# Another order of one unit's tiles, of its tails' preparation, and another issuer of one load

## The chip, the cores and the metric

The kernel runs on one core of one Trainium2 chip. The metric is the device time of one execution in microseconds; of the kernel before there are three runs, and their median is taken.

## The reference

Three stages follow one another. Attention has 4 batches, 8 heads, 576 positions and 64 elements a head, with a causal mask and a bias that decays with a cumulated sum. A sticky top-1 mixture of experts (512 inputs, 1024 hidden) and a gated convolution block with two further matrix products come behind it.

```
scores = scale * np.matmul(q, k.transpose(0, 1, 3, 2))
cum = np.cumsum(np.maximum(s, 0.0), axis=-1)
bias = -(cum[:, :, :, None] - cum[:, :, None, :])
scores = np.where(causal, -1000000000.0, scores + np.minimum(bias, 0.0))
attn = np.exp(scores - np.max(scores, axis=-1, keepdims=True))
attn = attn / (np.sum(attn, axis=-1, keepdims=True) + 1e-09)
x = np.matmul(attn, v)                      # heads beside one another
...
e = fresh_e if s == 0 or local_gate[b, s] < 0.5 else prev_e   # per token
out[b, s] = p[e] * (np.maximum(x[b, s] @ w1[e], 0.0) @ w2[e])
...
h = np.maximum(x @ w_in, 0.0)
y = (h * sigmoid(conv3(h, conv_w))) @ w_out
```

## The kernel before

The change touches attention alone, and there its beginning. The 32 pairs of batch and head are worked off as 8 units of 4 heads. Of the 576 positions 512 are the main part, laid out as transposed operands (`K1`, and `k2` in the second half of the contraction), and 64 are the tail, whose operands for all heads lie in `T1` and `T2`. Numbers are split into a high and a low float16 part, so a score tile is a sum of products of parts.

A unit has 14 score tiles (h, g). Tiles with g = 0, g = 1, and g = 2 of even heads need main operands only; g = 2 of odd heads and g = 3 need the tail operands as well. The order of the tiles of a unit is fixed: head 0 with g = 0, 1, 2, head 1 with g = 0 to 3, and the same for heads 2 and 3. Only unit 0 has an order of its own, the list `BEGIN`.

The main loop `for t in range(N + 9)` (L722) takes one tile a step. In step t it does what is planned for the step (`work`), the scores of tile t on PE into PSUM (L482, with masks L485), the pieces of the row maxima of a coming unit (`stage_a`: PE L382, then DVE L385 or, for tails, L413), the exps of tile t − 1 on ACT (`weights`: L521, or L526 and L527), the low part of the weights of tile t − 2 on DVE (`plo`, L538), and products with V four steps behind the last tile of a head (`values`, L554, started for an odd head by its tile g = 3, for an even one by g = 2). Output of a pair of heads is normalised, split and stored five to seven steps behind, and turned on PE by identity matmuls 10, 12 and 14 steps behind the tiles (1, 3) and (3, 3) (`turn_tile`, PE L914, emptied by ACT L915).

Row maxima are needed before the scores of a unit: PE turns them (L450, `max_turn`), ACT scales them (L455), and a DMA writes them into an operand row. They and `turn_tile` use the PSUM pool `mps`, which has one buffer; the pieces have two (`aps`), score tiles three (`zps`).

What is prepared ahead is planned by the table `PAR`: each name in `start` has a step, negative ones come before the loop, and equal steps go by the fraction. The names of the tails' chain are `thk`, `thq` (high parts, ACT), `tlk`, `tlq` (low parts, DVE L293), `ttk`, `ttq` (turned on PE L298, out by L301 on ACT and L303 on DVE), `ct` (copies into T1, DVE L327), `xt` (three operand rows, DMA), `pt` (the tail pieces of unit 0's maxima), `mtt`, `mot`, `mrt` (the maxima turned, scaled and written; `mrt` is a DMA on ACT's queue, L465). For unit 1: `hk1`, `hq1`, `lk1`, `lq1` (splits, ACT L259 and DVE L265), `T1k`, `T1q` (DMA transposes L277 on SP), `x1`, and its copies (L285, DVE) in `copies`; in `u1`, `sv` is the split of V, `pa` and `pn` the first step of the pieces and the number of steps they are spread over. `lk2`, `lq2` load q and k of unit 2, whose splits run on ACT (L259) and POOL (L267, L268). `lv0` and `lv1` load the two halves of V of batch 0 (`loadv`, L176 and L180), `sv0` splits the first (ACT L342, DVE L346, POOL L337 to L350), `c2` writes constants (POOL L205), `z` writes zeros.

Every engine, and SP's and POOL's queues too, works in the order in which the program issues, and waits at an instruction until its operands are there.

Of the kernel before, what the change touches and what calls it, by code (L numbers as in the profile page):

```python
# [42 lines left out]
class Keep:  # L43
# [3 lines left out]

PAR = {'u1': {'sv': -6, 'pa': -6, 'pn': 4, 'mx': -3},  # L50
 'u2': {'at': (-22, -21, -19, -18.9, -18), 'cp': (-14, -13), 'lv': -11, 'sv': -2, 'pa': -12, 'pn': 7, 'mx': -6},
 'u3': {'load': -35, 'loadq': 0, 'at': (-33, -30, -28, -27, -26.9), 'cp': (-22, -21), 'sv': -1, 'pa': -20, 'pn': 14, 'mx': -6},
 'u': {'load': -51,
# [34 lines left out]
           'hk1': -17,  # L88
           'mob': -16,
           'mrb': -15,  # L90
           'tlk': -14,
           'tlq': -13,
           'lk1': -12,
           'xt': -11,
           'T1k': -10,
           'ttk': 2.0,
           'ttq': 3.0,
           'hq1': 3.05,
           'lq1': 3.06,
           'T1q': 3.07,  # L100
           'x1': 3.08,
           'lk2': 3.09,
           'lq2': 3.095,
           'ct': 4.0,
           'pt': 4.1,
           'c2': 4.5,
           'mtt': 5.0,
           'mot': 5.1,
           'mrt': 5.2,
           'sv0': 5.4,  # L110
           'z': 6.0,
           'lv1': 6.1},
 'r': {'cut': 12, 'w1': 6, 'w2': 8, 'w3': 22},
 'm': 'faafaafaafaa'}


BEGIN = ([(0, 0), (0, 1), (1, 0), (1, 1), (0, 2), (1, 2), (1, 3)],
         [(0, 0), (0, 1), (1, 0), (1, 1), (2, 0), (2, 1), (0, 2), (1, 2), (1, 3), (3, 0), (3, 1), (2, 2), (3, 2), (3, 3)])


def attention(tc, ctx, q, k, v, s, xd, rt, hook):
# [8 lines left out]
    V, A, PE, Q, G = nc.vector, nc.scalar, nc.tensor, nc.sync, nc.gpsimd  # L130

    def pool(n, b, on=ctx, **kw):
        return on.enter_context(tc.tile_pool(name=n, bufs=b, **kw))

    const, vp, natv = pool("const", 1), pool("vv", 2), pool("natv", 1)
    p0p, php, wk, xp, xtp = pool("p0", PAR["h"]["p0"]), pool("phl", PAR["h"]["ph"]), pool("wk", 2), pool("xs", 2), pool("xt", 1)
    zps, aps, ops, mps = (pool(n, b, space=PSUM) for n, b in (("zps", 3), ("aps", 2), ("ops", 2), ("mps", 1)))
# [23 lines left out]
    def load(u, n):  # L161
        b, h0 = u // (H // NH), u % (H // NH) * NH
        t = big[n == "q"][:, 0:1024] if u % 2 == 0 else big[1][:, 1024 + 1024 * AT[n]:2048 + 1024 * AT[n]]
        t = U[u, n] = t.rearrange("p (h c d) -> p h c d", h=NH, c=2)
        for c in range(2):
            Q.dma_start(t[:, :, c], src[n][b, h0:h0 + NH, 256 * c:256 * c + 256].rearrange("h (p t) d -> p h (t d)", t=2))

    def loadv(b, part=None, D=Q):
        if part in (None, 0):
            U[b, "v"] = natv.tile([128, H, 4, 64], F32, name="nv")  # L170
            U[b, "vt"] = natv.tile([128, H // 2, 64], F32, name="nvt")
        w, wt = U[b, "v"], U[b, "vt"]
        h = slice(0, H) if part is None else slice(NH * part, NH * part + NH)
        for j in range(4):
            for t in range(2):
                D.dma_start(w[64 * t:64 * t + 64, h, j], v[b, h, 128 * j:128 * j + 128].rearrange("h (p t) d -> t p h d", t=2)[t])  # L176
        for e in range(2):
            for t in range(2):
                r = 64 * e + 32 * t
                D.dma_start(wt[r:r + 32, h.start // 2:h.stop // 2], v[b, h, 512:576].rearrange("(r e) (p t) d -> e t p r d", e=2, t=2)[e, t])  # L180
# [93 lines left out]
    def turn(u, e, ns=slice(0, 2)):  # L274
        if (u, 2) not in U:
            U[u, 1], U[u, 2] = K1[u % 3], st2.tile([128, 2, 2, 1024], F16, name="k2")
        Q.dma_start_transpose(out=U[u, 2][:, e, ns].rearrange("d n (x p) -> d (n x) p", p=64), in_=U[u, "h"][64 * e:64 * e + 64, ns].rearrange("p n x y d -> p (n x y d)"))  # L277
# [34 lines left out]
    def turn_tail(n, js, engines):  # L312
        for j, copy in zip(js, engines):
            turned(ht, AT[n], j, lambda z, j: (T2[:, :, AT[n], 128 * j:128 * j + 128].rearrange("d b (x p) -> d b x p", p=32), z.rearrange("d (x b p) -> d b x p", x=4, b=B)), copy)
# [14 lines left out]
    def split_v(u):  # L329
        b, o = u // 2, u % 2 * NH  # L330
        a, t = U[b, "v"][:, o:o + NH], U[b, "vt"][:, o // 2:o // 2 + 2]
        w = U[u, "vv"] = vp.tile([128, NH, 4, 2, 65], F16, name="vv")
        wt = U[u, "vvt"] = vp.tile([128, NH // 2, 2, 65], F16, name="vvt")
        v0 = U[u, "v0"] = vp.tile([128, NH, 65], F32, name="v0")
        for x in (w, wt):
            i = (slice(None),) * (len(x.shape) - 2)
            G.memset(x[i + (0, slice(64, 65))], 1.0)  # L337
            G.memset(x[i + (1, slice(64, 65))], 0.0)
        G.memset(v0[:, :, 64:65], 1.0)
        for x, dh, dl in ((a, w[:, :, :, 0, 0:64], w[:, :, :, 1, 0:64]), (t, wt[:, :, 0, 0:64], wt[:, :, 1, 0:64])):  # L340
            if u == 0 or not PAR["h"]["vg"]:
                A.activation(dh, x, AF.Copy, scale=VS)  # L342
            else:
                G.tensor_scalar(dh, x, VS, 0.0, op0=ALU.mult, op1=ALU.add)
            if u == 0:
                V.scalar_tensor_tensor(dl, in0=x, scalar=VS, in1=dh, op0=ALU.mult, op1=ALU.subtract)  # L346
            else:
                G.tensor_scalar(x, x, VS, 0.0, op0=ALU.mult, op1=ALU.add)
                G.tensor_tensor(dl, x, dh, op=ALU.subtract)
        G.tensor_scalar(v0[:, :, 0:64], a[:, :, 0], VS if u == 0 else 1.0, 0.0, op0=ALU.mult, op1=ALU.add)  # L350
# [93 lines left out]
    def max_turn(u, hs=slice(0, 4), tails=True):  # L444
        t = U[u, "mt"] = mps.tile([128, 512], F32, name="mt")
        r = span(hs, tails)
        x = mxs[u][:, 0:18] if hs == slice(0, 4) else mxs[u][:, 16:18]
        if hs and not tails:
            x = mxs[u][:, 4 * hs.start:4 * hs.stop]
        PE.matmul(t[0:r.stop - r.start, 0:128], lhsT=x, rhs=ident, start=True, stop=True, skip_group_check=True)  # L450

    def max_out(u, hs=slice(0, 4), tails=True):
        n = span(hs, tails).stop - span(hs, tails).start
        mr = U[u, "mr", key(hs)] = wk.tile([18, 128], F16, name="mr")
        A.activation(mr[0:n], U[u, "mt"][0:n, 0:128], AF.Copy, scale=2.0 ** -12)  # L455

    def max_row(u, hs=slice(0, 4), tails=True):
        n, Q = 0, nc.sync if u or hs else nc.scalar
        if hs:
            n = 4 * (hs.stop - hs.start)  # L460
            for e in range(2):
                Q.dma_start(U[u, 1][70:71, e, 1, 256 * hs.start:256 * hs.stop].rearrange("o (x c) -> o x c", c=128), U[u, "mr", key(hs)][n // 2 * e:n // 2 * e + n // 2])
        if tails:
            c = 256 * (u % 2)
            Q.dma_start(T1[70:71, u // 2, 1, c:c + 256].rearrange("o (r c) -> o r c", r=2), U[u, "mr", key(hs)][n:n + 2])  # L465
# [3 lines left out]
    def mode(x):  # L469

        m = PAR["m"][3 * x[1] + x[2]] if x[2] < 3 else "a"
        return "a" if m == "b" and x[0] < 3 else m
# [131 lines left out]
    def store(u, part):  # L604
# [3 lines left out]
        xh, eng = U[u, "xh"][:, part], G if u < NU - 1 else V  # L608
        if eng is G and PAR["h"]["xg"]:
            G.tensor_copy(xh[:, :, 0], x)  # L610
# [40 lines left out]
    copy(0, "q")  # L651
    load_tail("q")
    load(1, "k")
    todo, pieces, copies = {}, {}, {6: [(1, "k")], 7: [(1, "q")]}

    def plan(t, f):
        todo.setdefault(math.floor(t), []).append((t, len(todo), f))
# [13 lines left out]
    def second_a(r):  # L671
# [8 lines left out]
        pa=begin_a, mt0a=lambda: max_turn(0, first, False), mo0a=lambda: max_out(0, first, False), mr0a=lambda: max_row(0, first, False),  # L680
        ttk=lambda: turn_tail("k", range(4), "AVAV"), ttq=lambda: turn_tail("q", range(4), "AVAV"),
        pb=lambda: second_a(range(6, 8)), pc=lambda: second_a(range(8, 10)), pd=lambda: second_a(range(10, 12)),
        mtb=lambda: max_turn(0, second, False), mob=lambda: max_out(0, second, False), mrb=lambda: max_row(0, second, False),
        xt=extra_tail, ct=copy_tail, ldq1=lambda: load(1, "q"), lk2=lambda: load(2, "k"), lq2=lambda: load(2, "q"),
        T1k=lambda: [turn(1, e, slice(0, 1)) for e in range(2)], T1q=lambda: [turn(1, e, slice(1, 2)) for e in range(2)], x1=lambda: extra(1),
        pt=lambda: second_a(range(12, 15)), mtt=lambda: max_turn(0, None), mot=lambda: max_out(0, None), mrt=lambda: max_row(0, None),
        sv0=lambda: split_v(0), lv1=lambda: loadv(0, 1),
        z=lambda: Q.dma_start(xd[NT:NT + 128].rearrange("p (j c) -> p j c", c=256), bc(zero[:, None, 0:256], [128, 4, 256])))
    for n, t in PAR["start"].items():
        plan(t, begin_tasks[n])  # L690
# [3 lines left out]
    PER = len(seq)  # L694
    begin = BEGIN[PAR["h"]["bg"]]
    steps = [(u, *x) for u in range(NU) for x in (seq if u else begin + seq[len(begin):])]
# [881 lines left out]
```

## Time and profile before

| | |
|---|---|
| median of 3 runs | 713.57 us (713.11 to 715.43) |
| profiled execution | 710.43 us |
| its span, first to last instruction | 708.7 us, mean granted clock 0.942 |
| PE busy | 643.1 us, 91% of the span |
| DVE, ACT, POOL busy | 452.1, 390.5, 249.6 us |

Busy times are sums over the span. PEclk is the TensorE clock that the throttle granted, as a share of 2.4 GHz. In a timeline the brackets behind a row give how long the engine was idle before it and what it was released by; DVE, ACT and POOL work while PE does, so their waits matter where a row of PE names them.

### The profile page before, as it was taken

To read this page: it belongs to the slowest core of one execution; us is meant where nothing else is said; L and a number is where in the kernel's file an instruction comes from. 1 tells how busy PE (TensorE), PEld (TensorE's weight loads), DVE (VectorE), ACT (ScalarE), POOL (GpSimd) and SP (SyncE) were. 2 spreads that over 40 slices of the span, in tenths; PEclk is the share of its full clock that TensorE was granted. 3 is DMA by queue.
4 is the path that set the end of the run, shared out by engine and by line. 5 is a ranking of instruction groups with operands and counts; after the bars stand their busy time and mean duration, and the time that the engine had idled before them with its cause. 6 is when DMAs were issued, how large, how long until landed. Compare 5 with 4: busy or idle time off the path is not lost. (4 is left out here: it accounts for less than half of the span.)

```text
span 708.7 us, 15489 instructions
## 1 busy us (share of the span) xinstructions
PE 643.1 (91%) x5177; PEld 401.2 (57%) x5177; DVE 452.1 (64%) x859; ACT 390.5 (55%) x660; POOL 249.6 (35%) x356
## 2 busy tenths in 40 slices
PE   5668899899999566999998999999889999999997
PEld 2346778688888433444443444444367766665443
DVE  7874978988875699653885866753039985546000
ACT  5544667788788754743755563532049974645111
POOL 7456866654441059832344363333100000000000
PEclk9855989999999769999999999999999999999999
DMA  5767784756646445899999999963195000000111
GB/s 131 136 164 150 127 178 75 172 104 108 191 139 217 127 139 190 246 320 257 256 295 248 300 206 260 204 147 65 50 172 97 1 16 22 25 31 30 45 50 55
DMA packets 168828, 101.82 MB, mean 144 GB/s; under 512 B 119712, under 2 KB 147016, under 8 KB 168732
## 3 DMA queue, kind: packets, MB, share of 16 engines
q1 hardware_dynamic: 164744, 88.65, 52.2%
q0 software_dynamic: 3984, 11.99, 5.6%
q8 instruction: 47, 0.77, 0.5%
q14 instruction: 49, 0.40, 0.2%
q10 hardware_dynamic: 4, 0.00, 0.0%
HBM read 62.18 MB, written 15.31 MB: 109 GB/s over the span
## 5 line engine op out<-in xcount | busy, mean ns | idle before, releaser
L1188 PE MATMUL hp<-r,xt 128*128 x504 | 115.4, 387 | 7.9 <-ACT xt L1219 7.9
L1188 PE MATMUL yp<-r,ht 128*128 x504 | 112.2, 379 | 1.7 <-PEq L1295 1.7
L1386 PE MATMUL hp<-yt,wi 128*128 128x288 f16 x768 | 95.6, 286 | 2.5 <-DMA yt<-yd 2.5
L1434 PE MATMUL o<-wo,g 128*128 128x512 f16 x432 | 94.5, 379 | 0.0
L1188 PEld LDWEIGHTS <-xt 128*128 128x128 f16 x504 | 50.0, 99 | 69.3 <-ACT xt L1219 8.6
L1386 PEld LDWEIGHTS <-wi 128*128 128x128 f16 x768 | 75.1, 98 | 23.3 <-DMA yt<-yd 2.7
L1188 PEld LDWEIGHTS <-ht 128*128 128x128 f16 x504 | 48.5, 98 | 57.4 <-issue 1.8
L1144 DVE SCALAR_TENSOR_TENSOR r<-st,r 128x512 f32 (+3 forms) x80 | 70.7, 951 | 6.7 <-ACT r L1133 5.1
L1434 PEld LDWEIGHTS <-g 128*128 128x128 f16 x432 | 42.3, 98 | 49.5
L1133 ACT ACTIVATE r<-st 128x512 f32 (+3 forms) x84 | 57.1, 764 | 21.8 <-SPq L1181 16.8
L385 DVE TENSOR_REDUCE mx<-za 128x1 f32<-128x384 f32 (+4 forms) x97 | 57.0, 602 | 17.7 <-PE za L382 17.0
L1249 POOL DMA_INDIRECT yd<-ys,idx x21 | 23.6, 1122 | 125.6 <-DVEq L1172 77.6
L526 ACT ACTIVATE phi<-z,lnes 128x512 f16<-128x512 f32 (+1 forms) x80 | 50.6, 633 | 25.9 <-PE z L485 25.6
L482 PE MATMUL z<-k 71*128 71x128 f16 (+2 forms) x320 | 53.6, 294 | 8.5 <-ACT p L521 3.2
L538 DVE TENSOR_TENSOR plo<-z,phi 128x512 f16<-128x512 f32 (+1 forms) x80 | 48.2, 603 | 12.3 <-ACT z L527 11.7
L1403 DVE SCALAR_TENSOR_TENSOR c<-hb,cw,c 128x576 f32<-128x576 f32 x32 | 26.1, 816 | 35.3 <-ACT c L1397 35.3
L527 ACT ACTIVATE z<-z,lnes 128x512 f32<-128x512 f32 (+1 forms) x80 | 48.6, 607 | 0.0
L554 PE MATMUL o<-v,p 128*128 128x65 f32 x256 | 46.1, 293 | 0.0
L1437 ACT ACTIVATE s<-o 128x512 f32<-128x512 f32 x18 | 10.7, 597 | 63.1 <-PE o L1434 63.1
L1247 ACT ACTIVATE ys<-yp,pp 128x512 f16<-128x512 f32 x21 | 14.4, 685 | 53.5 <-PE yp L1188 32.3
L554 PE MATMUL o<-vv,phi 128*128 128x65 f16 (+1 forms) x512 | 42.7, 204 | 0.0
L554 PEld LDWEIGHTS <-phi 128*128 128x128 f16 x544 | 42.1, 110 | 0.0
(285 smaller groups left out, 1193.5 us busy)
## 6 DMA issues: line engine op xcount, KB each, us to landing
st<-in_moe_w_dram SPq DMA_DIRECT2D x8, 2048.0 KB
st<-in_moe_w_dram SPq DMA_DIRECT2D x24, 512.0 KB
out_dram<-s SPq DMA_DIRECT2D x18, 256.0 KB
st<-in_k_dram SPq DMA_DIRECT2D x16, 256.0 KB
st<-in_q_dram SPq DMA_DIRECT2D x16, 256.0 KB
xd<-xh SPq DMA_DIRECT2D x16, 256.0 KB
k<-in_moe_w_dram SPq DMA_DIRECT2D x8, 512.0 KB
s<-in_moe_w_in_dram SPq DMA_DIRECT2D x16, 256.0 KB
```

The source lines that it names most:

```text
L385: return lambda: V.tensor_reduce(out, z.rearrange("p (e c) -> p e c", e=m), axis=AX.X, op=ALU.max)
L482: PE.matmul(out, lhsT=ks[i], rhs=qs[i], start=first and not i, stop=False, skip_group_check=True)
L526: A.activation(hi[:, 0:n], z[:, 0:n], AF.Exp, bias=lnes, scale=1.0 / SC)
L527: A.activation(p[:, 0:n], z[:, 0:n], AF.Exp, bias=lnes, scale=1.0 / SC)
L538: (V if md == "a" else G).tensor_tensor(lo[:, 0:n], p[:, 0:n], hi[:, 0:n], op=ALU.subtract)
L554: PE.matmul(out, lhsT=w, rhs=x, start=first, stop=last, skip_group_check=True)
L1133: i = self.nc.scalar.activation(hi, src, AF.Copy, scale=self.scale[w])
L1144: i = nc.vector.scalar_tensor_tensor(lo, in0=src, scalar=sc, in1=hi, op0=ALU.mult, op1=ALU.subtract)
L1188: i = self.nc.tensor.matmul(out, lhsT=lhsT, rhs=self.rings[w][:, c, k, bass.ds(s, 1), f], **kw)
L1386: PE.matmul(st[x][:, n, 0:HN], lhsT=wi[:, c, k, m], rhs=t[:, n, a + k], start=k + a + c == 0, stop=k == 3 and a == 4)
L1403: V.scalar_tensor_tensor(c, in0=h[:, 1:S + 1], scalar=cw[:, m, 1:2], in1=c, op0=ALU.mult, op1=ALU.add)
L1434: PE.matmul(o, lhsT=g[:, a, k, 128 * i:128 * i + 128], rhs=wo[:, c, k], start=j == 0, stop=j == 23)
```

## The change

Three lists are changed, and one argument of a call.

- Unit 0's order: (3,0), (3,1) and (2,2) come forward from steps 9, 10 and 11 to 7, 8 and 9; (1,2) and (1,3), which need the tails, go from 7 and 8 to 10 and 11. (3,2) and (3,3) stay at 12 and 13.
- The tails' chain: the low parts go from before the loop to step 1, the turns and the copy one step later (3, 4, 5), the tail pieces from 4.1 to 6.1, the turned maxima from step 5 to 7. `hq1` to `lq2` move from step 3 to step 2. `sv0` stays at 5.4.
- Unit 1: its pieces are spread over steps 7 to 11 in place of 8 to 11, its V is split a step later, its two copies come a step earlier; its half of V is loaded by POOL ahead of the loop in place of by SP in step 6.

```diff
-PAR = {'u1': {'sv': -6, 'pa': -6, 'pn': 4, 'mx': -3},
+PAR = {'u1': {'sv': -5, 'pa': -7, 'pn': 5, 'mx': -3},
...
-           'ct': 4.0,
-           'pt': 4.1,
...
+           'ct': 5.0,
            'sv0': 5.4,
...
+           'pt': 6.1,
...
-         [(0, 0), (0, 1), (1, 0), (1, 1), (2, 0), (2, 1), (0, 2), (1, 2), (1, 3), (3, 0), (3, 1), (2, 2), (3, 2), (3, 3)])
+         [(0, 0), (0, 1), (1, 0), (1, 1), (2, 0), (2, 1), (0, 2), (3, 0), (3, 1), (2, 2), (1, 2), (1, 3), (3, 2), (3, 3)])
...
-    todo, pieces, copies = {}, {}, {6: [(1, "k")], 7: [(1, "q")]}
+    todo, pieces, copies = {}, {}, {5: [(1, "k")], 6: [(1, "q")]}
...
-        sv0=lambda: split_v(0), lv1=lambda: loadv(0, 1),
+        sv0=lambda: split_v(0), lv1=lambda: loadv(0, 1, G),
```

The order on ACT, around the scaling of the tails' maxima (`mr<-mt 2x128`) and its DMA; `vv` is the split of V of unit 0, `h<-st_111` and `h<-st_112` are the splits of k and q of unit 2, and `p`, `phi` and `z` exps. Before:

```order
L527 ACTIVATE z<-z,lnes 128x512
L455 ACTIVATE mr<-mt 2x128
L465 DMA t_141<-mr 1x2x128
L342 ACTIVATE vv<-nv 128x16x64
L342 ACTIVATE vvt<-nvt 128x2x64
L521 ACTIVATE p_578<-z,lnes 128x512
L259 ACTIVATE h<-st_111 128x16x64
L526 ACTIVATE phi<-z,lnes 128x512
L527 ACTIVATE z<-z,lnes 128x512
L259 ACTIVATE h<-st_112 128x16x64
```

After:

```order
L527 ACTIVATE z<-z,lnes 128x512
L342 ACTIVATE vv<-nv 128x16x64
L342 ACTIVATE vvt<-nvt 128x2x64
L521 ACTIVATE p_569<-z,lnes 128x512
L259 ACTIVATE h<-st_111 128x16x64
L526 ACTIVATE phi<-z,lnes 128x512
L527 ACTIVATE z<-z,lnes 128x512
L259 ACTIVATE h<-st_112 128x16x64
L455 ACTIVATE mr<-mt 2x128
L465 DMA t_141<-mr 1x2x128
```

The scaling went from ahead of the split of V to behind the second split of unit 2.

On DVE, from the copy of the turned tails (`t_142`) into T1 (`t_141`) on; `k_139` the operand of unit 1, `mx` the row maxima (`ISA` is the fused one of the tails). Before:

```order
L327 COPY t_141<-t_142 64x4x512 x2
L385 TENSOR_REDUCE mx<-za 128x2
L413 ISA za,mx<-za,zero,mx 128x512
L413 ISA mx 128x1
L413 ISA za,mx<-za,zero,mx 128x512
L413 ISA mx 128x1
L346 SCALAR_TENSOR_TENSOR vv<-nv,vv 128x16x64
L346 SCALAR_TENSOR_TENSOR vvt<-nvt,vvt 128x2x64
L538 TENSOR_TENSOR plo<-z,phi 128x512
L285 COPY k_139<-k_426 64x2x1024
L538 TENSOR_TENSOR plo<-z,phi 128x512
```

After:

```order
L327 COPY t_141<-t_142 64x4x512 x2
L346 SCALAR_TENSOR_TENSOR vv<-nv,vv 128x16x64
L346 SCALAR_TENSOR_TENSOR vvt<-nvt,vvt 128x2x64
L538 TENSOR_TENSOR plo<-z,phi 128x512
L285 COPY k_139<-k_424 64x2x1024
L385 TENSOR_REDUCE mx<-za 128x2
L413 ISA za,mx<-za,zero,mx 128x512
L413 ISA mx 128x1
L413 ISA za,mx<-za,zero,mx 128x512
L413 ISA mx 128x1
L285 COPY k_139<-k_424 64x2x1024
L538 TENSOR_TENSOR plo<-z,phi 128x512
```

The tails' row maxima stood ahead of the split of V (`vv`) and of both copies of unit 1; now they stand behind the split and the first copy.

On ACT, at the scaling of unit 2's maxima (`mr<-mt 18x128`), step 23 of the loop; `xT<-mt` empties a group of turned output tiles. Before:

```order
L915 ACTIVATE xT<-mt 128x4x128
L521 ACTIVATE p_1294<-z,lnes 128x512
L455 ACTIVATE mr<-mt 18x128
L526 ACTIVATE phi<-z,lnes 128x512
L527 ACTIVATE z<-z,lnes 128x512
L526 ACTIVATE phi<-z,lnes 128x512
L527 ACTIVATE z<-z,lnes 128x512
L915 ACTIVATE xT<-mt 128x4x128
L521 ACTIVATE p_1415<-z,lnes 128x512
```

After:

```order
L521 ACTIVATE p_1287<-z,lnes 128x512
L915 ACTIVATE xT<-mt 128x4x128
L455 ACTIVATE mr<-mt 18x128
L526 ACTIVATE phi<-z,lnes 128x512
L527 ACTIVATE z<-z,lnes 128x512
L526 ACTIVATE phi<-z,lnes 128x512
L527 ACTIVATE z<-z,lnes 128x512
L915 ACTIVATE xT<-mt 128x4x128 x2
L521 ACTIVATE p_1415<-z,lnes 128x512
```

Where one `xT` followed four exps, two now do; the turns that fill the one PSUM buffer for them stand back to back on PE.

## Rows read from the trace of the kernel before

**Rows 1.** Windows: busy us of each engine, PEclk the granted clock, DMA share, GB/s.

```profile
30.00:47.00 17.00, 8.93 (x60) 5.13 (x59) 11.66 (x18) 9.83 (x16) 3.98 (x3) 0.51 0.81 163
47.00:64.00 17.00, 14.26 (x90) 9.98 (x91) 10.44 (x23) 4.21 (x8) 13.41 (x18) 0.50 0.79 164
64.00:71.00 7.00, 7.00 (x66) 6.00 (x65) 2.38 (x7) 4.21 (x10) 4.57 (x8) 0.50 0.38 93
71.00:84.00 13.00, 11.89 (x168) 10.41 (x167) 11.66 (x26) 10.34 (x20) 11.50 (x18) 0.99 0.79 120
...
88.00:95.00 7.00, 6.34 (x37) 4.11 (x36) 4.18 (x11) 3.64 (x7) 6.08 (x23) 0.52 0.78 154
```

**Rows 2.** PE's timeline, 24:64 us: start, us, what; idle before it <- releaser.

```profile
28.38 0.59 PE L482 MATMUL z<-k 71*128 71x512 f16 x2 [1.68 <-DVE t L303]
...
34.80 0.32 PE L382 MATMUL za<-t 70*64 70x64 f16 x4 [1.94 <-DVE t L327]
...
41.86 1.01 PE L482 MATMUL z<-k 71*128 71x256 f16 x4 [2.60 <-ACT p L521]
...
56.04 0.58 PE L382 MATMUL za<-k 70*128 70x512 f16 x1 [1.13 <-DVE mx L385]
...
63.83 0.40 PE L450 MATMUL mt<-ident,mx 128*18 128x128 f32 x1 [1.14 <-DVE mx L413]
```

**Rows 3.** ACT's timeline, 38 to 54 us.

```profile
38.12 0.27 ACT L455 ACTIVATE mr<-mt 2x128 f16<-2x128 f32 x1 [3.99 <-PE mt L450]
...
41.14 0.67 ACT L521 ACTIVATE p<-z,lnes 128x512 f32<-128x512 f32 x1
41.80 1.06 ACT L259 ACTIVATE h<-st 128x1024 f16<-128x1024 f32 x1
...
44.59 1.06 ACT L259 ACTIVATE h<-st 128x1024 f16<-128x1024 f32 x1 [0.60 <-DMA st<-in_q_dram]
...
53.52 1.06 ACT L259 ACTIVATE st<-st 128x1024 f16<-128x1024 f32 x1 [5.59 <-DMA st<-in_k_dram]
```

**Rows 4.** DVE's timeline, 31 to 72 us.

```profile
31.49 1.22 DVE L265 SCALAR_TENSOR_TENSOR st<-st,st 128x1024 f16<-128x1024 f32 x1
...
41.07 1.23 DVE L346 SCALAR_TENSOR_TENSOR vv<-nv,vv 128x1024 f16<-128x1024 f32 x1 [3.63 <-ACT vv L342]
...
43.12 1.40 DVE L285 COPY k<-k 64x2048 f16<-64x2048 f16 x1
...
71.74 0.69 DVE L285 COPY k<-k 64x2048 f16<-64x2048 f16 x1
```

**Rows 5.** SP's queue, 27 to 48 us: its issues.

```profile
27.93 8.09 SPq L277 DMA_TRANSPOSE k<-st  x4
...
40.71 5.36 SPq L176 DMA_DIRECT2D nv<-in_v_dram  x8
46.12 2.01 SPq L180 DMA_DIRECT2D nvt<-in_v_dram  x4
```

**Rows 6.** POOL's timeline, 16 to 43 and 72 us.

```profile
16.38 4.94 POOL L176 DMA_DIRECT2D nv<-in_v_dram  x8
...
22.18 1.60 POOL L180 DMA_DIRECT2D nvt<-in_v_dram  x3 [0.32 <-DMA nv<-in_v_dram]
...
42.94 1.04 POOL L267 TENSOR_SCALAR st<-st 128x1024 f32<-128x1024 f32 x1 [16.28 <-ACT h L259]
...
72.03 1.30 POOL L267 TENSOR_SCALAR st<-st 128x1024 f32<-128x1024 f32 x1 [1.52 <-ACT h L259]
```

**Rows 7.** PE's timeline around unit 2's maxima, 90 to 94 us.

```profile
90.52 0.61 PE L450 MATMUL mt<-ident,mx 128*18 128x128 f32 x2
...
93.18 1.06 PE L482 MATMUL z<-k 71*128 71x512 f16 x2
```

**Rows 8.** ACT's timeline, the same stretch.

```profile
91.17 0.27 ACT L455 ACTIVATE mr<-mt 18x128 f16<-18x128 f32 x1 [5.20 <-PE mt L450]
...
93.63 0.57 ACT L915 ACTIVATE xT<-mt 128x512 f16<-128x512 f32 x1
```

More of the change, by code (lines that the diff above doesn't have):

```diff
@@ L90 @@
            'mrb': -15,
[L91 to L103, printed above, removed]
-           'ct': 4.0,
-           'pt': 4.1,
[L106 to L109, printed above, removed]
-           'sv0': 5.4,
-           'z': 6.0,
-           'lv1': 6.1},
+           'lk1': -14,
+           'xt': -13,
+           'T1k': -12,
+           'lv1': -11,
+           'tlk': 1.05,
+           'tlq': 1.06,
+           'hq1': 2.05,
+           'lq1': 2.06,
+           'T1q': 2.07,
+           'x1': 2.08,
+           'lk2': 2.09,
+           'lq2': 2.095,
+           'ttk': 3.0,
+           'ttq': 4.0,
+           'ct': 5.0,
+           'sv0': 5.4,
+           'c2': 5.5,
+           'pt': 6.1,
+           'z': 6.2,
+           'mtt': 7.0,
+           'mot': 7.1,
+           'mrt': 7.2},
  'r': {'cut': 12, 'w1': 6, 'w2': 8, 'w3': 22},
```

## The prediction

> **What bounds the kernel now.** I read the windows first. At full clock PE is nearly saturated (11.89 of the 13 us from 71, at 0.99 [rows 1]), so what can be won lies where it waits or runs at half clock, and one stretch has both: at the start of the main loop the granted clock is 0.51 from 30 to 47 us and 0.50 up to 71 [rows 1], the lower level, 1.2 GHz. 0.51 over 17 us puts the fall at about 30.3 us, and 0.99 over the 13 us from 71 puts the return at about 71.3. PE works 8.93 of the 17 us up to 47, 14.26 of the next 17 and all 7.00 of the last 7. There is one more low stretch near: 0.52 over 88 to 95 [rows 1].
>
> Then PE's timeline, for what its gaps there end on. Between 28 and 64 us it has nine gaps over 0.5 us, 12.3 us together; the first, the last and three between them are [rows 2]. Three wait for DVE's casts of the turned tails (first: 1.68). 1.94 wait for DVE's copy into T1 (L327), 2.60 for an exp of ACT (L521); the rest for `plo`, a copy of k and row maxima (1.13 before the last, 1.14 at the last).
>
> Third, ACT. The 2.60 is made there: ACT stands 3.99 us at L455, the scaling of the tails' maxima, and all that is queued behind it is late, the exp L521 at 41.14 too, on which PE's gap at 41.86 ends [rows 2, 3].
>
> **The change part by part.**
>
> *Tails' chain later, tail tiles later.* The tail pieces go from right behind the copy L327 to two steps later, so the 1.94 goes. L455 on ACT moves behind the split of V, one exp and both splits of unit 2, so the exp of 41.14 no longer stands behind it: the 2.60 goes. What is late next is on DVE: the tails' row maxima, which stood ahead of the split L346 and the copy L285, now stand behind them, and PE's transposition of the maxima and the two PSUM buffers of the pieces wait for those. By rows 1.23 + 1.40 = 2.63 [rows 4]; at best nothing of it, if PE has score tiles enough meanwhile. I take all of it, since two buffers are soon full. The copy's duration is where a rule bears: one copy took 1.40, starting just after POOL's L267 had begun; a like one took 0.69, starting before POOL's next L267 [rows 4, 6]. The Trainium skill, "SBUF — State Buffer" (Who interferes with whom), says that VectorE's copies of that kind and GpSimd share a port pair which one instruction holds to its end. The rows agree as far as they go. By it the copy, now ahead of POOL's L267, costs 0.69 and the give-back is 0.7 us smaller.
>
> *Unit 1's pieces over five steps.* Fourteen pieces from step 7 (3, 3, 3, 3, 2) instead of from step 8 (4, 3, 4, 3). Of the last two row-max gaps, 2.27 us, between none and all goes; I take a third, −0.76, because the pieces stay behind one another on DVE in the same number.
>
> Together: −1.94 − 2.60 + 2.63 − 0.76 = −2.7 us of PE waiting before unit 1's maxima are turned. Ends: −6.8 (nothing given back, both gaps gone) and +0.7 (the 2.60 stays, no row-max gap goes). What that is worth depends on the clock. If full clock returns as much earlier as the work does, the whole counts; if it returns at 71.3 whatever happens, work is brought forward at half speed and the gain is half, −1.35. PE's last gap before the return ends at 63.83, with full work after it [rows 1, 2], which speaks for a return that follows the work. I take −2.4.
>
> *The other order of unit 0's tiles* has a consequence later. Units' finished output is turned on PE into one PSUM buffer, which ACT empties (L915). (1,3) now stands at step 11 and (3,3) at 13; their turns, 12 and 10 steps behind, fall into the same step, 23. Eight turns stand back to back, the second four wait for L915, and that stands on ACT behind L455 of unit 2 and four exps. At that place before, PE began L450 at 90.52 and its next score tile at 93.18, and ACT's chain from L455 at 91.17 ended with L915 at 94.20 [rows 7, 8]. So PE would have waited 94.20 − 93.18 = 1.0 us there. That was at half clock; at full clock PE's 2.66 us would be 1.33, while ACT's chain of 3.68 from 90.52 stays: 2.3 us. Behind PE's wait stand the next score tiles, so all of it counts. ACT had a wait for PE soon after in any case. I take +1.5, nearer to the half-clock row, since that stretch is at 0.52.
>
> *Unit 1's V issued by GpSimd.* Twelve issues leave SP, 5.36 + 2.01 = 7.4 us [rows 5], and join POOL: eight cost it 4.94 and three of the tails 1.60, so some 7.1 us [rows 6]. They lie in POOL's idle 16.28 us before L267; even with twice the price 2 us are left. SP's 7.4 us had made unit 3's load late, for which ACT stood 5.59 us at 53.52 [rows 3]; that goes. But PE's gap near it ended on DVE's row maxima [rows 2], so it is worth 0. V of unit 1 comes earlier than needed. The cost if that cover fails (POOL late for L267): 0 on PE, as POOL's half of unit 2's split is needed by a copy only at 71.74 [rows 4].
>
> Sum: −2.4 + 1.5 = −0.9 us. The profiled execution took 710.43 us (span 708.7 and 1.7 outside) and would become 709.5. The median of the runs is 713.57, 3.1 above it; on that scale I forecast 712.7. Own range of this case: −2.7 + 1.0 = −1.7 to −1.35 + 2.3 = +1.0, so 711.9 to 714.6.
>
> **Rivals.**
>
> *The clock returns earlier.* The fuller work from 34 to 47 us may bring back full clock before the last stretch: 64 to 71 ran at 0.50 with PE busy throughout, and at full clock its 7 us are 3.5. Then −2.7 − 3.5 + 2.3 (step 23 at full clock) = −3.9: 709.7. For it: busy PE, and a return which came after unbroken work. Against: pieces and tiles still wait for DVE, and from 47 to 64 us 14.26 of 17 busy did not bring it. The Trainium skill, "TensorE: Matmul & The Clock Gate" (Part 1), has the half rate as the default, which activity releases; the trace agrees in that the return followed 7.00 of 7.00 busy. Chance 0.22.
>
> *The wait moves to the next load.* With L455 out of the way ACT comes early to L259, the split of unit 2's k, and stands there for its load, with the same exps behind it as before. That load is on SP behind four transposes of 8.09 us [rows 5]. Before, L259 ran at 41.80 without a wait, and the next split stood 0.60 us for its load [rows 3], so loads are hardly early. The transposes' second pair waited for DVE's L265, done at 32.71 [rows 4]; two took 36.02 − 32.71 = 3.31 from there, the first two the same from 27.93, so without that wait SP is free 1.5 us earlier at most. The 2.60 then returns less 1.5 = 1.1: −2.7 + 1.1 + 1.5 = −0.1, 713.5, no change. Against it: the exp on which PE's gap ended is queued ahead of L259. Chance 0.18.
>
> *Slower.* The doubled turn at step 23 falls into a stretch that is at half clock already [rows 1]. A wait of 2.3 us within it can put off the return: half as long again as its 7 us, 3.5 us at half clock, costs 1.7. With the gain halved: −1.35 + 2.3 + 1.7 = +2.65, 716.2. It decides from the point at which step 23's wait and what it does to the clock exceed the gain left. For it: one PSUM buffer and ACT's row of exps ahead of L915 are certain. Against: PE worked 6.34 of those 7 us and the clock still was low, so it isn't only its waits. Chance 0.15.
>
> **How the numbers follow.** Forecast 0.45, rivals 0.22, 0.18, 0.15. A measurement of this kernel can tell about 0.3%, 2.1 us, from no change: below 711.4 is faster, above 715.7 slower. Faster: nearly all of the first rival, 0.20, and 0.09 from the unused end (−6.8) of the forecast's first term: 0.29. Slower: 0.11 of the last rival and 0.04 from the upper ends of the others: 0.15. Same 0.56. The range runs from just under the first rival's 709.7 to the slower one's 716.2: 709.2 to 716.3.
>
> **What would show it.** Right, if in the profile after: L455 of the tails waits for nothing long and PE's gap on L521 near 41 us is gone; the 1.94 before the tail pieces is replaced by a wait for DVE of 1 to 3 us at them; ACT's 5.59 at L259 is gone and PE no better for it; V is issued by POOL within its idle time; and PE stands 1 to 2.3 us at its second group of L914 for ACT. Wrong, if the clock's return moves by several us against the work in either direction, if PE's gap at step 23 is under 0.5 us, or if later units change by more than step 23 brings.

## The result and the profile after

The changed kernel takes 716.50 us, the median of 20 runs (710.26 to 721.11); the kernel before took 713.08 in 20 runs of the same measurement (704.29 to 717.19). The ratio is 1.0074, 95% interval 1.0046 to 1.0102: slower, where 712.7 and no change were forecast, and 0.2 us above the range. The ratio leaves out runs more than 1.5% above a kernel's fastest, and before has one very fast run; that is why it says 5.3 us where the medians stand 3.4 apart. The means of all runs lie 4.1 us apart (95% interval 2.3 to 6.0). The profiled execution took 717.90, its span 715.8.

The windows of the same stretches as in [rows 1], after (stretch, length, busy us by engine, granted clock, DMA share, GB/s):

```profile
30.00:47.00 17.00, 10.36 (x82) 6.99 (x82) 11.52 (x20) 7.94 (x14) 6.94 (x12) 0.75 0.97 201
47.00:64.00 17.00, 14.28 (x118) 10.65 (x116) 9.95 (x22) 8.81 (x17) 14.10 (x20) 0.50 0.57 97
64.00:71.00 7.00, 7.00 (x63) 6.33 (x61) 3.31 (x7) 3.40 (x7) 6.84 (x9) 0.50 0.87 158
71.00:84.00 13.00, 11.53 (x147) 9.60 (x145) 10.89 (x24) 8.06 (x17) 10.55 (x25) 0.93 0.70 132
88.00:95.00 7.00, 5.32 (x38) 3.93 (x38) 3.12 (x8) 4.31 (x8) 5.35 (x7) 0.63 0.63 71
```

The clock falls later than before (0.75 instead of 0.51 over the first 17 us), but it comes back later too (0.93 instead of 0.99 over the 13 us from 71), and the second low stretch, which by the record of the granted clock had run from 88.3 to 95.1 us, runs from 89.8 to 100.1. PE's gaps there, answering to [rows 2] (in brackets the idle time and its releaser):

```profile
29.46 0.38 PE L298 MATMUL z<-id,k 128*128 128x128 f16 x4 [2.02 <-DVE t L303]
...
34.25 0.25 PE L382 MATMUL za<-t 70*64 70x64 f16 x4 [0.88 <-DVE t L327]
...
37.30 0.64 PE L382 MATMUL za<-k,t 70*64 70x512 f16 x2 [2.30 <-DVE mx L385]
...
45.21 0.40 PE L382 MATMUL za<-k 70*128 70x256 f16 x2 [3.04 <-DVE mx L385]
...
48.94 0.48 PE L382 MATMUL za<-k 70*128 70x256 f16 x2 [1.20 <-DVE mx L385]
...
60.41 0.61 PE L450 MATMUL mt<-ident,mx 128*18 128x128 f32 x2 [1.16 <-DVE mx L413]
```

The 1.94 before the tail pieces is 0.88, and the 2.60 behind L521 is gone. 2.30 between the tail pieces and 3.04 before a piece of unit 1 have come in their place. Two stretches show where the time went. Between the last row maxima of unit 0's main part and the turning of unit 1's (L450), first before, then after:

```profile
24.27:63.83 39.56, 26.77 (x194) 17.76 (x194) 27.06 (x44) 17.91 (x30) 19.70 (x28) 0.58 0.72 147
```

```profile
24.42:60.41 35.99, 24.30 (x194) 16.54 (x194) 25.38 (x44) 18.48 (x30) 25.06 (x39) 0.70 0.82 166
```

PE stood 39.56 − 26.77 = 12.8 us before and 35.99 − 24.30 = 11.7 after; the stretch is 3.6 us shorter, mostly because less of it ran at half clock (0.70 against 0.58). And from unit 2's L450 to unit 3's, before and after:

```profile
90.52:114.89 24.37, 23.60 (x322) 19.67 (x321) 18.91 (x46) 18.34 (x34) 15.64 (x20) 0.91 0.64 121
```

```profile
88.98:116.98 28.00, 25.91 (x324) 22.09 (x324) 18.77 (x46) 18.93 (x35) 14.77 (x19) 0.82 0.49 86
```

Unit 1's maxima are turned 3.4 us earlier than before (60.41 for 63.83), unit 2's 1.5 us earlier (88.98 for 90.52), unit 3's 2.1 us later (116.98 for 114.89). Those 3.6 us between units 2 and 3 turned the gain of this part into a loss; what is lost behind it, the experiments take up.

### The profile page after: what moved, and what is told of

It reads as the page before. It is cut to its first block, busy times and chain, and to the rows that moved or that the text cites. A ratio compares the mean times of both kernels' runs of the same rounds, so it can differ in the third digit from the quotient of the medians.

```text
span 715.8 us, 15493 instructions
## 1 busy us (share of the span) xinstructions
PE 645.4 (90%) x5177; PEld 405.5 (57%) x5177; DVE 451.1 (63%) x859; ACT 391.2 (55%) x660; POOL 256.6 (36%) x368
## 5 line engine op out<-in xcount | busy, mean ns | idle before, releaser
L1386 PE MATMUL hp<-yt,wi 128*128 128x288 f16 x768 | 98.0, 291 | 5.1 <-DMA yt<-yd 5.1
L1434 PE MATMUL o<-wo,g 128*128 128x512 f16 x432 | 94.5, 379 | 0.0
L526 ACT ACTIVATE phi<-z,lnes 128x512 f16<-128x512 f32 (+1 forms) x80 | 50.6, 632 | 32.6 <-PE z L485 29.7
L1249 POOL DMA_INDIRECT yd<-ys,idx x21 | 21.7, 1033 | 124.9 <-DVEq L1172 87.5
L554 PE MATMUL o<-v,p 128*128 128x65 f32 x256 | 48.0, 301 | 0.0
L554 PE MATMUL o<-vv,phi 128*128 128x65 f16 (+1 forms) x512 | 44.3, 208 | 0.0
L554 PEld LDWEIGHTS <-phi 128*128 128x128 f16 x544 | 43.9, 113 | 0.0
```

The source lines that it names most:

```text
L526: A.activation(hi[:, 0:n], z[:, 0:n], AF.Exp, bias=lnes, scale=1.0 / SC)
L554: PE.matmul(out, lhsT=w, rhs=x, start=first, stop=last, skip_group_check=True)
L1386: PE.matmul(st[x][:, n, 0:HN], lhsT=wi[:, c, k, m], rhs=t[:, n, a + k], start=k + a + c == 0, stop=k == 3 and a == 4)
L1434: PE.matmul(o, lhsT=g[:, a, k, 128 * i:128 * i + 128], rhs=wo[:, c, k], start=j == 0, stop=j == 23)
```

## The experiments

Each ran 12 times beside 17 to 35 runs of the kernel before. Their ratios to it:

| | median, us (before on that chip) | ratio, 95% interval |
|---|---|---|
| turns apart | 714.39 (713.67) | 1.0000, 0.9964 to 1.0037 |
| V on SP | 716.23 (713.67) | 1.0013, 0.9978 to 1.0049 |
| order alone | 715.85 (713.67) | 1.0030, 0.9999 to 1.0062 |
| tails at step 9 | 714.95 (713.67) | 0.9990, 0.9952 to 1.0028 |
| fill | 714.04 (712.58) | 1.0034, 0.9997 to 1.0070 |
| before, double turn | 715.79 (712.58) | 1.0028, 0.9993 to 1.0063 |
| k early | 710.73 (712.58) | 0.9975, 0.9935 to 1.0014 |
| k early, V's split later | 713.15 (712.58) | 1.0005, 0.9969 to 1.0042 |
| k early, V on SP | 711.63 (712.60) | 0.9987, 0.9964 to 1.0011 |
| before, V on GpSimd | 714.36 (712.60) | 1.0027, 0.9998 to 1.0056 |
| k early, again | 712.95 (712.60) | 0.9965, 0.9928 to 1.0002 |
| fill at the start | 712.21 (711.35) | 1.0004, 0.9974 to 1.0034 |

No interval is clear of 1 by itself, so single times decide little here. Weighted together by their intervals, the three experiments with the doubled turn (V on SP; order alone; before, double turn) stand at 1.0024 (1.0005 to 1.0044), the seven of the changed kernel without the doubled turn and without the fill at step 23 at 0.9990 (0.9978 to 1.0003); experiments on one chip share the runs of the kernel before, so this is rough. The traces decide more, but there is one of each kernel, and they do not repeat exactly. "k early" and "k early, again" are the same program: unit 1's maxima are turned at 59.67 and 59.44 us, unit 2's at 84.83 and 86.29, and from there to unit 3's it takes 22.4 and 24.4 us, as one had no low stretch there and the other had one from 83.6 to 90.4. Up to step 23 the changed kernel, "turns apart" and "fill" are one program too, and unit 1's maxima come at 60.41, 61.10 and 61.67.

**Turns apart** (`e1_turn_apart`).

```diff
-            y = at(d)
+            y = at(13 if n == 1 and t < 2 * PER else d)
```

> The changed kernel, with one edit: the second group of turned output tiles of unit 0's first pair comes 13 instead of 12 steps behind its tile, so in step 24, alone, instead of in step 23 beside another group. Theory A (the doubled turn of step 23 makes the loss): PE's wait of 1.31 us for L915 at the second group goes, the second low stretch of the clock falls from 10.2 to about 7 us, unit 3's maxima are turned 2 to 3.5 us earlier than in the changed kernel (113.5 to 115 instead of 117.0), and the median falls by as much, to 713 to 714.5. Rival B (V issued by GpSimd makes it): nothing changes beyond 0.5 us. Rival C (where the clock falls is chance, no single edit does it): the wait goes, 1.3 us, and the low stretches come out anyhow.

The wait for L915 is gone and unit 3's maxima are turned at 113.72 us, 3.3 earlier than in the changed kernel; from unit 2's to unit 3's maxima:

```profile
89.79:113.72 23.93, 23.16 (x325) 19.45 (x324) 18.90 (x46) 18.87 (x35) 14.24 (x19) 0.93 0.58 106
```

The low stretch was not shorter, it lay earlier (82.8 to 93.1 by the clock's record); of the expected signs that one failed. The fall at 82.8 lies ahead of the edited step, so it is not the edit's doing, and part of the 4.1 us that this stretch is shorter by (28.00 to 23.93) may be owed to it. The median is 2.1 us under the changed kernel's, and 0.7 above the kernel before where the changed kernel was 3.4 above.

**V on SP** (`e2_v_on_sp`).

```diff
-           'lv1': -11,
...
+           'lv1': 6.3,
...
-lv1=lambda: loadv(0, 1, G),
+lv1=lambda: loadv(0, 1),
```

> The changed kernel, with unit 1's half of V issued by SP in step 6 again. Theory A (doubled turn): the times stay at those of the changed kernel within 1 us; ACT waits again several us for unit 3's load and PE does not. Rival B (12 more issues on GpSimd, and V's traffic beside the transposes, cost the time): 2 to 3.5 us faster than the changed kernel, 713 to 714.5, and ACT's wait of 6.61 us at the split of unit 2's k falls to under 5. Rival C: within 1 us of the changed kernel.

716.23, as theory A had it: by the medians moving V back gains nothing. Beside its own runs of the kernel before (1.0013, and 1.0074 for the changed kernel) a gain of some us is not excluded. Rival B's sign is absent: ACT still waits 6.55 us at the split of unit 2's k. ACT waits 4.45 us again at the split for unit 3's load, and PE has 2.03 us before a tail piece where the changed kernel has 0.25:

```profile
57.26 0.32 PE L382 MATMUL za<-t 70*64 70x64 f16 x4 [2.03 <-DVE mx L385]
```

```profile
54.53 0.32 PE L382 MATMUL za<-t 70*64 70x64 f16 x4 [0.25 <-DVE mx L385]
```

So the relief of SP is worth up to 1.8 us in front by these two rows. What stands against it, the run with V on GpSimd alone says.

**The order alone** (`e3_order_alone`): the kernel before with the new list `BEGIN`.

> The kernel before, with unit 0's new order of tiles alone. Theory A (doubled turn): it has the double turn of step 23 with its wait of 1 to 2.3 us, and PE still waits 1.9 us for the copy into T1 and 2.6 us for the exp behind the tails' maxima, so it keeps the loss and has no gain: 2 to 4 us slower than before, 715 to 717. Rival B (V on GpSimd): it equals the kernel before within 1 us. Rival C: between 0 and 2 us slower, by the wait alone.

715.85, 2.2 us above before, within theory A's forecast; 28.1 us between the maxima of units 2 and 3, with 0.9 us of waiting for L915:

```profile
92.11:120.19 28.08, 26.45 (x326) 22.23 (x325) 18.91 (x46) 18.91 (x35) 14.47 (x19) 0.80 0.47 91
```

**The tails at step 9** (`e4_tails_at_9`): the changed kernel with this order, and `at(11 if ...)` in the line of the first experiment.

```diff
-... (3, 0), (3, 1), (2, 2), (1, 2), (1, 3), (3, 2), (3, 3)])
+... (3, 0), (3, 1), (1, 2), (1, 3), (2, 2), (3, 2), (3, 3)])
```

> The changed kernel, with the tiles (1,2) and (1,3) at steps 9 and 10 and (2,2) at 11, and the second group of that pair's turned output 11 steps behind, at step 21, so that no step has two groups. Theory A (doubled turn): as with the turns set apart, 2 to 3.5 us under the changed kernel, 713 to 714.5. Rival B: as the changed kernel within 1 us. Rival C: 1.3 us under it, by the wait alone.

714.95, 0.45 us above A's forecast; 22.1 us between the maxima of units 2 and 3, all at full clock:

```profile
89.72:111.85 22.13, 21.36 (x320) 18.32 (x320) 18.74 (x46) 18.21 (x34) 14.26 (x19) 1.00 0.61 113
```

**Fill** (`e5_fill`): the changed kernel; PE works in its wait, the queue behind stays.

```diff
-        z = zps.tile([128, 512], F32, name="z")
+        z = st.pop("early", None) or zps.tile([128, 512], F32, name="z")
...
+                if t == 23 and n == 2:
+                    st["early"] = zps.tile([128, 512], F32, name="z")
+                    busy(st["early"], 5)
```

> The changed kernel, with five identity matmuls of 512 columns put between the two groups of turned tiles of step 23, into the PSUM buffer that the next score tile overwrites: PE works where it stood 1.31 us for L915, and everything behind it stays queued as before. Theory A1 (what costs is the clock: with PE standing there, the low stretch runs on to some 11 us behind unit 2's maxima): the stretch ends 3 to 7 us sooner after unit 2's maxima, the stretch from unit 2's to unit 3's maxima falls from 28.0 to 25 to 26 us, the median by 1 to 3 us under the changed kernel, 713.5 to 715.5. Rival A2 (what costs is the wait and the work behind it, whatever the clock does): 28 us or a little more stay, and the median at 716 to 717.

The five matmuls took 2.34 us of PE at half clock, more than the wait they cover. Nevertheless (L917 of this kernel is L914 of the others, L368 the fill):

```profile
91.79 0.63 PE L917 MATMUL mt<-unit,xh 128*128 128x128 f16 x4
92.21 2.34 PE L368 MATMUL z<-id 128*128 128x512 f16 x5
94.35 0.47 PE L917 MATMUL mt<-unit,xh 128*128 128x128 f16 x4
```

```profile
90.25:115.41 25.16, 24.39 (x330) 19.88 (x330) 18.79 (x46) 18.83 (x35) 14.79 (x19) 0.93 0.55 105
```

25.2 us with more work in it, instead of 28.0, and a low stretch from 91.1 to 94.5 in place of 89.8 to 100.1. The median of 714.04 is 2.5 under the changed kernel's; beside its own runs of the kernel before it is 1.5 above, not 3.4, but the ratio of 1.0034 does not show a gain. By the trace that is A1: not the 1.3 us of the wait make most of the loss, but the half clock that goes on behind it. The Trainium skill, "TensorE: Matmul & The Clock Gate" (Part 1), says that activity releases the throttle; this run agrees, 0.93 with the fill against 0.82 without.

**Before with the double turn** (`e6_before_double`): in the kernel before, `at(15 if n == 1 and t < 2 * PER else d)`.

> The kernel before, with one edit: the second group of turned output of unit 0's first pair 15 instead of 12 steps behind, so that it falls into step 23 beside the third group. Nothing else is changed. Theory A (the doubled turn makes the loss): unit 2's to unit 3's maxima take 27.5 to 28.5 us instead of 24.4, the low stretch ends some 11 us behind unit 2's maxima instead of 4.6, and the median is 2 to 3.5 us above before, 715.5 to 717. Rival B (the new order of tiles loses for another reason, late values or pieces): the wait is there, 1 us, and the median within 1.2 us of before.

Everything as theory A had it: 0.86 us of waiting, 28.4 us between the maxima, the end of the low stretch 11.8 us behind unit 2's maxima (102.7), the median 3.2 us above before.

```profile
93.16 0.63 PE L914 MATMUL mt<-unit,xh 128*128 128x128 f16 x4
94.66 0.58 PE L914 MATMUL mt<-unit,xh 128*128 128x128 f16 x4 [0.86 <-ACT xT L915]
```

```profile
90.94:119.31 28.37, 26.74 (x325) 22.50 (x324) 18.78 (x46) 18.91 (x35) 15.62 (x20) 0.79 0.57 102
```

**k early** (`e7_k2_early`): turns apart, and unit 2's k loaded before the second pair of transposes.

```diff
+           'lk2': 2.065,
            'T1q': 2.07,
            'x1': 2.08,
-           'lk2': 2.09,
```

> The changed kernel with the turns set apart, and unit 2's k loaded ahead of the second pair of transposes of unit 1 on SP in place of behind them. Theory D (the expected gain went into ACT's wait of 6.2 us for this load, behind which the exps stand, for those DVE's low part of the weights, and behind that the row maxima for which PE stood 2.8 us): ACT's wait falls to under 2 us, PE's gap of 2.81 us at 45 us to under 1, unit 1's maxima come 1.5 to 2.5 us earlier than with the turns set apart (58.6 to 59.6), and the median lies at 711.5 to 713.5. Rival E (PE's gap there is set by DVE's own queue): ACT's wait falls and PE's gap stays over 2 us; the median at 713.5 to 714.5.

The chain it is about, in the changed kernel, ACT and then DVE (answering to [rows 3, 4]):

```profile
34.34 0.70 ACT L521 ACTIVATE p<-z,lnes 128x512 f32<-128x512 f32 x1
41.65 1.06 ACT L259 ACTIVATE h<-st 128x1024 f16<-128x1024 f32 x1 [6.61 <-DMA st<-in_k_dram]
...
44.90 0.25 ACT L455 ACTIVATE mr<-mt 2x128 f16<-2x128 f32 x1
```

```profile
36.36 0.69 DVE L285 COPY k<-k 64x2048 f16<-64x2048 f16 x1
...
43.87 0.69 DVE L538 TENSOR_TENSOR plo<-z,phi 128x512 f16<-128x512 f32 x1 [4.44 <-ACT z L527]
44.48 2.07 DVE L385 TENSOR_REDUCE mx<-za 128x4 f32<-128x512 f32 x3
```

ACT stands 6.61 us at the split L259 for k of unit 2; the exps are queued behind it, `plo` on DVE waits 4.44 us for one, and the row maxima of unit 1 stand behind `plo`: PE's 3.04. With k early, ACT and PE:

```profile
37.56 1.06 ACT L259 ACTIVATE h<-st 128x1024 f16<-128x1024 f32 x1 [2.45 <-DMA st<-in_k_dram]
...
43.22 1.06 ACT L259 ACTIVATE h<-st 128x1024 f16<-128x1024 f32 x1 [3.47 <-DMA st<-in_q_dram]
```

```profile
37.38 0.64 PE L382 MATMUL za<-k,t 70*64 70x512 f16 x2 [2.42 <-DVE mx L385]
...
48.21 0.48 PE L382 MATMUL za<-k 70*128 70x256 f16 x2 [3.00 <-DVE mx L385]
...
59.67 0.61 PE L450 MATMUL mt<-ident,mx 128*18 128x128 f32 x2 [1.16 <-DVE mx L413]
```

ACT's wait for k falls to 2.45 and PE's gap at 45 is gone, but ACT now stands 3.47 us for q and PE 3.00 a piece later. Unit 1's maxima are 1.4 us earlier than with the turns apart: half of theory D. The median of 710.73 is lower than D's forecast, its interval still reaches over 1.

**V's split later** (`e8_k2_sv0`): on top, `sv0` at 6.15 in place of 5.4, behind `pt`.

> As the kernel with k of unit 2 loaded early, and the split of unit 0's V planned behind the tail pieces in place of ahead of them, so that DVE's L346 pair (1.5 us) and ACT's L342 stand behind the tails' row maxima. Theory D and the forecast's first step: PE's gap of 1.9 to 2.3 us between the tail pieces falls to about 0.5, and the median is a further 0.5 to 1.5 us lower, 710.5 to 713. Rival E: the 2 us return at the next piece, and the median is within 0.5 us of the run beside it.

PE's gap between the tail pieces fell from 2.42 to 0.41 us and came back as 3.27 at the next piece, for a copy of DVE (L285):

```profile
36.58 0.64 PE L382 MATMUL za<-k,t 70*64 70x512 f16 x2 [0.41 <-DVE mx L385]
...
43.26 0.61 PE L382 MATMUL za<-k 70*128 70x128 f16 x4 [3.27 <-DVE k L285]
```

Unit 1's maxima at 60.28, none earlier: rival E. The median was 2.4 us over that of the run beside it, more than E said, but not clear of the noise of 12 runs each.

**k early, V on SP behind unit 3's loads** (`e9_k2_v_sp`): `lk2` as above, `lv1` on SP at 7.3.

> The changed kernel with the turns set apart, k of unit 2 loaded early, and unit 1's half of V issued by SP again, now behind unit 3's loads. Theory F (V on GpSimd has a price at the far end: from the last write to yd to the first transposes of the last stage 7.19 us instead of 6.34, because POOL's four closing semaphore steps take 1.57 instead of 1.33 us each, and 4.4 instead of 3.95 us behind PE's last matmul): both go back to 6.34 and 3.95, 1.3 us, while unit 1's maxima stay within 1 us of the kernel with k early alone (59.7), as unit 3's loads no longer stand behind V. Median 709 to 711.5. Rival G (the far end is chance, and V on SP costs its 7 us in front again): the far end varies between both values, unit 1's maxima come at 61.5 or later, and the median is at 711.5 to 714.

**Before with V on GpSimd** (`e10_v_pool_alone`): in the kernel before `'lv1': -11` and `loadv(0, 1, G)`.

> The kernel before, with unit 1's half of V issued by GpSimd ahead of the loop, and nothing else. Theory F: 7.19 us from the last write to yd to the first transpose instead of 6.34, semaphore steps of 1.57 us, 4.4 us behind the last matmul; 1.3 us and up to 1 more of low clock there are lost; near the beginning PE gains at most 1 us, as its gap at 56 us ended on row maxima. Median 0.5 to 2 us above before. Rival G: 6.34 and 3.95, or a mixture, and the median within 0.5 us of before.

These two go together. The last stage reads `yd` through DMA transposes on SP; between POOL's last write to it and the first of them lie, in the kernel before:

```profile
507.22 0.97 POOL L1249 DMA_INDIRECT yd<-ys,idx  x1 [4.92 <-DVEq L1172]
```

```profile
513.56 5.59 SPq L1353 DMA_TRANSPOSE yt<-yd  x4
```

and with V on GpSimd as the only change:

```profile
507.74 0.97 POOL L1249 DMA_INDIRECT yd<-ys,idx  x1 [4.92 <-DVEq L1172]
```

```profile
514.93 5.50 SPq L1353 DMA_TRANSPOSE yt<-yd  x4
```

6.34 and 7.19 us. In between POOL makes four closing steps on its queue's semaphores; from the view of their line, before and with V on GpSimd (count, minimum, median and maximum in ns, first and last start):

```profile
L1330 POOLq INC_SWDGE_SEM  x4: 1335/1340/1357, 507.3 to 512.0; - x4
```

```profile
L1330 POOLq INC_SWDGE_SEM  x4: 1575/1575/1580, 507.8 to 513.2; - x4
```

4 × 0.235 = 0.94 us, of which 0.85 arrive. All eight profiles with V on GpSimd (the changed kernel, e1, e4, e5, e7, e8, e10, e11) have 7.19 or 7.20 us, all six with V on SP (before, e2, e3, e6, e9, e12) 6.34 or 6.35. From the end of PE's last matmul to the end of the span it is 4.40 to 4.51 us against 3.94 to 3.95, so another 0.45. Theory F stands in the traces, with 1.3 us. Of the times, e9 has the short values again, unit 1's maxima at 59.20, and the median at 711.63, a little above its forecast's upper end; e10's median is 1.75 us above before, within F's forecast, but its interval still touches 1, and it does not show the gain in front, though unit 1's maxima came 1.8 us earlier (62.02 for 63.83; the clock fell at 35.0 instead of 30.3).

**k early, again** (`e11_k2_again`).

> The kernel with the turns set apart and unit 2's k loaded early, once more, beside the two others on the same chip. Theory D: unit 1's maxima at 59 to 60.5 us, unit 2's to unit 3's maxima within 22 to 25 us, ACT's wait for k 2 to 3 us, the median 1 to 3 us under before. Rival C (chance of where the clock falls): median within 1 us of before.

Unit 1's maxima at 59.44, ACT's wait for k 1.07 (2 to 3 were expected), 24.4 us between the maxima of units 2 and 3; the median 0.35 us above before, the ratio 0.9965 and its interval still to 1.0002. Unit 1's maxima repeat, the gain in time is not shown.

**Fill at the start** (`e12_fill_start`): on e9, `busy` on free PSUM buffers, 4 and 2 before the last of the tails' turns, 5 before the last tail piece, 4 before a piece of unit 1.

> The kernel with turns apart, k early and V on SP behind unit 3's loads, and fifteen identity matmuls of 512 columns that compute nothing used, put on PE ahead of four instructions at which it stood: four and two before the last of the tails' turns, five before the last tail piece, four before a piece of unit 1. Theory H (much of the beginning's time hangs on the clock, which falls behind PE's gaps from 28 to 48 us): the low stretch that began at 35.2 us and lasted 37.6 us is 10 us or more shorter, unit 2's maxima come 2 to 6 us earlier (84 to 88 instead of 90.2), median 707 to 710.5. Rival I (the low stretch is set by what PE does in the whole stretch, and fifteen short matmuls do not move it): the stretch is as long, the added work costs 1 to 3 us at unit 1's maxima (60 to 62), median 711.5 to 714.

Nearer to rival I: the low stretch began at 42.2 instead of 35.2 us, which neither had, but ended at 72.9 as it had (72.8), unit 1's maxima came at 60.23 instead of 59.20, the median at 712.21, and the next low stretch was longer, 17 us (83.2 to 100.3). It is also the one kernel without a double turn that took long from unit 2's to unit 3's maxima:

```profile
91.25:117.87 26.62, 25.86 (x325) 21.93 (x325) 18.90 (x46) 18.88 (x35) 13.72 (x19) 0.83 0.52 104
```

PE stands only 0.8 us in it. So a low stretch of 9.0 us behind unit 2's maxima, without the wait, took 2.2 us more than before's 24.4, where the double turn took 3.6 to 4.0 more; and low stretches there can grow for other reasons as well.

## Why the prediction was wrong

**The doubled turn (+1.5).** This is the step that failed. The wait was sized rightly: 1.31 us, within 1.0 to 2.3. What the sum left out, and gave as the slower rival with 0.15, is the clock behind it: between unit 2's and unit 3's maxima 3.6 us were lost, where +1.5 was taken. PE at step 23 of the changed kernel, and ACT, answering to [rows 7, 8]:

```profile
88.98 0.38 PE L450 MATMUL mt<-ident,mx 128*18 128x128 f32 x2 [0.16 <-DVE mx L413]
...
90.52 0.63 PE L914 MATMUL mt<-unit,xh 128*128 128x128 f16 x4
92.47 0.58 PE L914 MATMUL mt<-unit,xh 128*128 128x128 f16 x4 [1.31 <-ACT xT L915]
```

```profile
91.85 0.57 ACT L915 ACTIVATE xT<-mt 128x512 f16<-128x512 f32 x1
```

From unit 2's to unit 3's maxima the four kernels with a double turn take 28.0, 28.0, 28.1 and 28.4 us; the eight without one or a fill take 22.1 to 24.4. Filling the wait gives 25.2. By the record of the granted clock 10.2 to 11.8 us of it run at half clock with the double turn, 0 to 4.6 in the eight, 3.4 with the wait filled; only the fill at the start lies between, with 9.0 of 26.6 us. PE stands 1.6 to 2.1 us there with the double turn and 0.8 without. And the four medians with it, 715.79 to 716.50, lie above those of the ten without it or with it filled, 710.73 to 714.95, though these are from several chips. The turns set apart gain 2.1 us by medians, the double turn added to before costs 3.2: that is the loss. Over before's 24.4 the two stretches are 3.6 and 4.0 us longer, of which 1.3 and 0.9 are the wait and 2.3 and 3.1 half clock.

The wait did not begin the low stretch, which in all four kernels began ahead of it. It put off its end: 11.0 to 11.8 us behind unit 2's maxima, 4.6 us in the kernel before and 4.3 with the wait filled. Adding the turn to before and filling the wait show that, with one trace each. The rival's working (1.7 us for a stretch half as long again) was near; its chance was far too low. It was set by how busy PE had been in that stretch before, not by the first low stretch, in which the return (71.3) came only after PE's last gap (63.83).

**The tails' gaps (−2.7, taken −2.4).** The two gaps named did go, and the give-back of 2.63 came as 2.30 at the tail pieces. But the 2.60 returned as 3.04, along the chain of the second rival: ACT's wait for unit 2's k moved up by the time that L455 had held it. The objection to that rival, that the exp of 41.14 stands ahead of L259, was true and beside the point, since the next exps stand behind. PE's standing fell by 1.1 us instead of 2.7. That unit 1's maxima came 3.4 us earlier is mostly the clock, which fell at 35.2 instead of 30.3; the edit need not have made that, as it fell at 29.7 in the kernel with the fill, the same program there. More than half of it was lost again: the return did not follow the work, it came at 72.7 instead of 71.3 (0.93 over the window from 71), so the first rival did not come about either. At unit 2's maxima 1.5 us were left of the 2.4.

**The copy and the shared port.** The first copy of unit 1 took 0.69 us at 36.36, with POOL idle up to 42.79; the row that the sum took, with POOL at work, said 1.40. This agrees with what the Trainium skill, "SBUF — State Buffer" (Who interferes with whom), says of a port pair shared by the two, though a copy beside an idle POOL does not test who holds it. The give-back was smaller, in part for it (2.30 for 2.63), but no time was won: PE's next gap, 3.04, ended on row maxima behind `plo`, which waited for ACT until 43.87.

**V on GpSimd (0).** Its own step was right: 5.00 + 2.26 = 7.3 us of issues (7.1 forecast), with 9.86 us of POOL's idle time left before L267, and ACT's 5.59 [rows 3] gone. POOL, answering to [rows 6]:

```profile
23.22 5.00 POOL L176 DMA_DIRECT2D nv<-in_v_dram  x8
28.09 2.26 POOL L180 DMA_DIRECT2D nvt<-in_v_dram  x4
...
42.79 1.05 POOL L267 TENSOR_SCALAR st<-st 128x1024 f32<-128x1024 f32 x1 [9.86 <-ACT h L259]
```

The 0 was wrong at both ends: up to 1.8 us won in front (the row of e2), 1.3 lost at the far end. By these two e2 should come out about level, as its median did; the medians cannot show a difference of this size. The price stood some 470 us behind the edited place, in a part that the trace of before shows and the prediction did not ask about.

**The sum.** By the traces the terms are −1.5 (up to unit 2's maxima, with what V won in front), +3.6 and +1.3, +3.4 us together, where −2.4 + 1.5 + 0 = −0.9 was forecast. The medians stand 3.4 apart as well; that it fits to the tenth is luck, with one trace of each.

Of the 7.1 us between the two profiled spans 2.1 stand at unit 3's maxima and 1.3 at the far end. The other 3.7 are not explained by the edit: from unit 3's maxima to the end of the span the two traces of the one program "k early" take 602.6 and 595.5 us.

What remains open: whether the half clock at the start can be shortened (its end lay between 66.0 and 75.8 us in these kernels, in none of them tied to one edit), and why the second low stretch was so long behind the fill at the start.

## What to carry to other kernels

Before shifting work by steps, list what else lands in the target step by its fixed offsets; two users of one PSUM buffer in a step make PE wait, and here a wait of 0.9 to 1.3 us in a stretch at half clock went with 3.6 to 4.0 us more. A wait that is removed on an engine with an ordered queue is to be followed to the next load on that queue before its gain is booked. When instructions move to another DMA queue, look also at the places where that queue's semaphores are closed and drained, however far away.

## What the hardware showed unexpectedly

POOL's closing steps on its queue's semaphores took 1.34 us each in the kernels with V on SP and 1.58 in those with twelve more DMA issues on GpSimd, to 0.02 us the same in every profile; three earlier steps of the kind (L1290) took 1.25 to 1.26 and 1.49 to 1.50. What in the count or the place of those issues sets this was not tried. Five matmuls that compute nothing, in a wait that they more than filled, shortened the stretch from 28.0 to 25.2 us.
